# One transformer block on one core: a hand-written instruction order laid out anew

## The chip, the core and the metric

The kernel runs on one core of one Trainium2 chip. Five engines of the core appear below: PE (matrix products; its weight loads are shown as a row of their own, PEld), DVE (vector work), ACT (activation functions), POOL (here only constants) and SP (which issues every DMA). The metric is device time in microseconds. The kernel before was run three times: 169.81, 170.02 and 170.82 us, median 170.02.

## What is computed

A block of two sublayers over x of 2048 rows and 512 columns, in bfloat16. The first sublayer normalises x, forms q, k, v, and does linear attention with 32 heads of 16 columns. The second normalises the result and applies a two-layer network with a ReLU.

```python
phi = lambda t: jnp.where(t > 0, t + 1, jnp.exp(t)) + 1e-6
pq, pk = phi(q), phi(k)
kv  = einsum("bhsd,bhse->bhde", pk, v)
z   = einsum("bhsd->bhd", pk)
o   = einsum("bhqd,bhde->bhqe", pq, kv) / (einsum("bhqd,bhd->bhq", pq, z) + 1e-6)
h   = x + o @ wo                       # q, k, v = layernorm(x) @ wqkv
out = h + relu(layernorm(h) @ w1) @ w2 # w1: 512 x 1792, w2: 1792 x 512
```

## The kernel before

Rows are cut into 16 tiles of 128 rows (t = 0 to 15) and 4 chunks of four tiles (c = 0 to 3). PSUM has 8 banks, and every matrix product names the bank it goes to. Nothing plans the work: a string, ORDER, lists 547 words, and the program emits one small function for each word in the order of the string. A word is a name and its numbers; for products the bank is among them. Each engine runs its own words in the order in which they stand; words of different engines meet only through semaphores, where one reads what another wrote or overwrites what another reads. So an order is a queue for each engine, and a word that must wait holds everything behind it on its engine. SP's queue is one of them: loads, transposing DMAs and stores stand in one line.

```python
for word in ORDER.split():
    name, *idx = word.split(".")
    ops[name](*map(int, idx))
```

The stages and the names that are used below (lines of the profile in brackets):

- **Start.** `lx.t.n` loads n tiles of x, `lk`, `lq`, `lv`, `lo`, `l1`, `l2` load parts of the weights (first number: where the part begins, second: how many slices; all on SP, L201 and L204). `warm` and `warmf` are filler products on zeros (L215, L221). `const` and `masks` fill constants, `table` loads ACT's function table.
- **First normalisation.** `S.t` statistics (DVE, L237), `A.t` aggregates them (DVE, L238), `R.t.n` computes 1/sqrt on ACT (two activations, L243 and L244), `N.t` normalises the tile (DVE, L262). The tile is then transposed, for tiles 0 to 3 by PE (`T.t`, L281) and an ACT copy out of PSUM (`E.t`, L291), for the others by a DMA from SP (`X.t`, L302).
- **Keys.** `K.t` is four products of 512 columns (L310; a word with two more numbers is a half of it). phi is made from them by `F` (exp, ACT), `U` (relu, ACT), `M` (minimum, DVE, L335) and `D` (sum, DVE, L338); for the last pair of tiles `W` takes U's and D's place. `G.t` (PE, L362) accumulates normalised-x-transposed times pk in banks 4 to 7 over all tiles, four products a tile, one a bank. The key sum z is accumulated by DVE in `za`, finished by `zf` (L373 to L375), and brought into columns by small products `z.j` (L381), copied by `zc`, spread by `zh`. The G sums are copied by `gA`, and `kv`, `kx`, `m`, `mA` form one 512 x 512 matrix out of wv, kv and wo.
- **Queries.** `Q.c.j` (L318), with `qF`, `qU`, `qM`, `qD`, `qW` as for keys.
- **Division.** `dn.c` (PE, L459) forms the denominators of a chunk, `dnl` and `dnx` (ACT, L465 and L472) their reciprocals, spread over columns. These are transposed by DMA (`dt.t`, L491, SP), one tile of the first two chunks by PE (`rt`, with `rv` or `re`). `dm` (DVE, L495) multiplies them into the queries, `h.t` (PE, L505) applies the matrix, `hD.t` (DVE, L511) adds x.
- **Second normalisation.** `s`, `a`, `r`, `n` (L239, L240, L243, L269) and the transposes `x.t` (SP, L303), one by PE (`t`, `e`). The division by the deviation is put off to the end.
- **Feed-forward.** `p.c.f` (PE, L521) makes one of 14 slices of the hidden layer for a chunk, four products; `pA` (ACT, L527) or `pD` (DVE, L532) applies the ReLU to a pair of banks. `f.t` (PE, L541) is 14 products of a tile with w2, mostly emitted as two words of seven. `fo.t` (DVE, L549) scales and adds h, `fd.t` (SP, L556) stores. Tile 15 is cut into three pieces by columns.

Of the kernel before, what the change touches and what calls it, by code (L numbers as in the profile page):

```python
# [38 lines left out]
p.0.10.3 hD.8 dt.15 s.8 a.6 pD.0.6.2 a.4 pA.0.10.2 n.6 f.1.1.0.7 hD.9 n.7 f.1.1.7.7 s.9 dm.3.0.2 dm.3.2.2 h.11.7  # L39
a.5 n.5 h.12.2 h.15.6 h.14.4 fo.1 h.10.5 hD.11 f.0.7.0.7 hD.12 x.6 a.8 h.13.1 a.9 f.3.3.0.7 f.3.3.7.7 x.7 hD.15  # L40
n.4 hD.14 f.0.7.7.7 x.4 f.2.0.0.7 hD.13 fo.3 x.5 p.1.0.6 s.12 s.11 n.8 hD.10 fo.0 p.1.1.7 a.11 fd.0 p.1.5.3 s.10
pD.1.0.2 f.2.0.7.7 a.12 n.12 n.9 s.14 p.1.4.2 n.11 p.1.8.4 fo.2 p.1.3.1 r.4.4 a.10 a.14 p.1.13.7 p.1.2.0
pD.1.4.2 n.10 x.10 x.11 s.13 p.1.7.2 p.1.9.5 p.1.12.6 a.13 pD.1.2.2 s.15 a.15 pD.1.8.2 n.14 pD.1.12.2 p.1.6.1
n.15 x.9 x.8 pA.1.6.2 f.7.0.0.7 p.1.10.4 fd.1 p.1.11.5 pD.1.10.2 fd.3 f.5.2.0.7 p.2.9.7 p.2.11.5 f.7.0.7.7
f.5.2.7.7 fo.7 p.2.8.6 p.2.10.4 p.2.5.1 pD.2.10.2 p.2.4.0 r.8.4 pA.2.8.2 f.4.4.0.7 fo.5 p.2.2.5 fd.2 pA.2.4.2
p.2.3.6 n.13 f.4.4.7.7 p.2.1.3 x.12 p.2.0.2 f.6.0.0.7 x.14 pA.2.2.2 fo.4 x.13 x.15 p.3.3.7 p.3.7.5 p.3.2.6
r.12.4 p.3.9.4 f.6.0.7.7 pA.2.0.2 p.3.11.1 p.3.8.3 p.3.4.2 fd.4 fd.5 fo.6 pA.3.8.2 pD.3.2.2 p.3.10.0 p.3.5.3
p.3.6.4 pA.3.10.2 fd.7 pA.3.6.2 p.2.6.6 pD.3.4.2 p.2.7.7 pD.2.6.2 p.3.13.5 p.3.1.1 fd.6 p.2.12.6 p.3.0.0
# [543 lines left out]
```

## Time and profile before

| what | us |
|---|---|
| three runs, median | 170.02 |
| the profiled execution, span from first to last instruction | 168.8 |
| PE busy, weight loads busy | 163.1, 78.0 |
| DVE busy, ACT busy, POOL busy | 104.4, 65.1, 4.8 |
| all products L521 (first layer), mean of one | 50.0, 0.379 |
| all products L541 (second layer) | 50.1 |

The profiled execution's own time is not listed apart from its span; the runs' median stands 1.2 us above the span. The granted PE clock is 1.000 over the whole span. In the profile a product's record is longer than the time for which it holds PE, since products are pipelined: a run of twelve shows 2.75 us. A row of the timeline begins with start and length in us from the start of the span; neighbouring instructions of one kind are merged, with their count behind an x. What stands in brackets at a row's end is idle time of the engine before it, and what ended it. The chain that ended last is followed back from the last instruction. In the views of one line, the row of DMA landings counts from the start of SP's issue.

### The profile page before, as it was taken

How to read it: one execution, taken by the hardware profiler on the slowest of the kernel's cores; microseconds unless marked ns; L12 is line 12 of the kernel's file. 1: busy time of each engine (PE TensorE's matmuls, PEld its weight loads, DVE VectorE, ACT ScalarE, POOL GpSimd, SP SyncE). 2: the span in 40 equal slices, each digit the busy share in tenths (PEclk: the TensorE clock that was granted, in tenths of full speed). 3: DMA queues.
4: the chain of work that ended last, by engine and by line, in shares of the span. 5: the costliest groups of instructions: out<-in, count | busy, mean ns of one | idle time of the engine just before them, and what ended most of it. 6: DMA issues, size and time to landing. Idle time of an engine off the chain costs nothing.

```text
span 168.8 us, 2286 instructions
## 1 busy us (share of the span) xinstructions
PE 163.1 (97%) x855; PEld 78.0 (46%) x871; DVE 104.4 (62%) x205; ACT 65.1 (39%) x97; POOL 4.8 (3%) x21
## 2 busy tenths in 40 slices
...
GB/s 112 352 245 97 97 66 124 176 270 378 174 64 65 77 138 87 134 62 95 37 62 0 31 31 122 126 4 0 62 93 0 31 0 4 0 0 93 0 65 94
DMA packets 30491, 15.49 MB, mean 92 GB/s; under 512 B 23184, under 2 KB 29328, under 8 KB 30480
## 3 DMA queue, kind: packets, MB, share of 16 engines
...
q8 instruction: 7, 0.11, 0.3%
...
HBM read 7.86 MB, written 2.10 MB: 59 GB/s over the span
## 4 chain that ended last, share of the span: by engine, by line
PE 85%; DVE 7%; DMA 4%; issue 1%; SPq 0%
PE bk L541 29%; PE bk L521 28%; PE bk L505 8%; PE bk L318 8%; PE bk L362 6%; PE bk L310 4%; DVE st L237 3%; DMA x_nat<-in_A_x_dram 2%; DMA lnT<-h_nat 2%; DVE h_nat L262 2%; PE bk L459 1%; DVE eb L335 1%; PE bk L403 1%; PE bk L415 1%; SPq L201 0%
## 5 line engine op out<-in xcount | busy, mean ns | idle before, releaser
L541 PE MATMUL bk<-w_sb,at 128*128 128x512 bf16 (+2 forms) x247 | 50.1, 355 | 0.3
L521 PE MATMUL bk<-lnT,w_sb 128*128 128x512 bf16 x219 | 50.0, 379 | 0.3
L527 ACT ACTIVATE at<-bk 128x1024 bf16<-128x1024 f32 x14 | 14.2, 1023 | 57.4 <-PE bk L521 57.4
L541 PEld LDWEIGHTS <-at 128*128 128x128 bf16 x252 | 23.6, 98 | 25.4 <-ACT at L527 0.3
L549 DVE SCALAR_TENSOR_TENSOR gT<-bk,rstd,h_nat 128x512 bf16<-128x512 f32 (+2 forms) x18 | 12.2, 689 | 35.7 <-PE bk L541 35.6
L521 PEld LDWEIGHTS <-w_sb 128*128 128x128 bf16 x224 | 21.8, 98 | 25.8
L532 DVE TENSOR_SCALAR at<-bk 128x1024 bf16<-128x1024 f32 x14 | 17.1, 1218 | 12.8 <-PE bk L521 12.6
L328 ACT ACTIVATE eb<-bk 128x1024 bf16<-128x1024 f32 (+1 forms) x18 | 16.6, 928 | 6.6 <-PE bk L310 4.8
L310 PE MATMUL bk<-wk_sb,lnT 128*128 128x512 bf16 x63 | 15.3, 380 | 0.4 <-ACT lnT L291 0.3
L505 PE MATMUL bk<-m_sb,pqs 128*128 128x512 bf16 x63 | 15.4, 380 | 0.1
L318 PE MATMUL bk<-lnT,wq_sb 128*128 128x512 bf16 x61 | 15.1, 379 | 0.1
L362 PE MATMUL bk<-at,h_nat 128*128 128x512 bf16 x55 | 13.5, 379 | 0.1
L331 ACT ACTIVATE rb<-bk 128x1024 bf16<-128x1024 f32 (+1 forms) x14 | 12.5, 904 | 0.3 <-PE bk L310 0.3
L511 DVE TENSOR_TENSOR h_nat<-bk,x_nat 128x512 bf16<-128x512 f32 x16 | 10.5, 680 | 2.9 <-PE bk L505 2.9
L237 DVE BATCH_NORM_STATS2 st<-x_nat 128x6 f32<-128x512 bf16 x16 | 10.8, 680 | 2.4 <-DMA x_nat<-in_A_x_dram 2.4
L239 DVE BATCH_NORM_STATS2 st<-h_nat 128x6 f32<-128x512 bf16 x16 | 10.7, 683 | 0.1
L310 PEld LDWEIGHTS <-lnT 128*128 128x128 bf16 x64 | 6.0, 98 | 8.4 <-ACT lnT L291 1.0
L362 PEld LDWEIGHTS <-h_nat 128*128 128x128 bf16 x64 | 6.2, 98 | 7.4 <-issue 0.2
L505 PEld LDWEIGHTS <-pqs 128*128 128x128 bf16 x64 | 5.9, 98 | 7.9 <-DVE pqs L495 1.8
L318 PEld LDWEIGHTS <-wq_sb 128*128 128x128 bf16 x64 | 5.9, 98 | 6.4
L472 ACT ACTIVATE wk_sb<-ld 128x1024 bf16<-128x1024 f32 x8 | 8.1, 1050 | 0.1
L335 DVE TENSOR_SCALAR eb<-eb 128x1024 bf16<-128x1024 bf16 (+1 forms) x18 | 6.8, 383 | 0.9 <-ACT eb L328 0.9
...
## 6 DMA issues: line engine op xcount, KB each, us to landing
out_dram<-gT SPq DMA_DIRECT2D x15, 128.0 KB, 1.9
...
```

The source lines that it names most:

```text
L237: op_S = lambda t: nc.vector.bn_stats(out=st[:, t, :], in_=x_nat[:, t, :])
L310: nc.tensor.matmul(bk[:, b, :], lhsT=lnT[c][:, kd, j * P : (j + 1) * P], rhs=wk_sb[:, kd, :], start=(kd == 0), stop=(kd == KD - 1),)
L318: nc.tensor.matmul(bk[:, b, :], lhsT=wq_sb[:, kd, j * P : (j + 1) * P], rhs=lnT[c][:, kd, :], start=(kd == 0), stop=(kd == KD - 1),)
L328: nc.scalar.activation(out=buf(eb, kind, i, n), in_=bank(at_bank[kind, i], n), func=ACT.Exp)
L331: nc.scalar.activation(out=buf(rb, kind, i, n), in_=bank(at_bank[kind, i], n), func=ACT.Relu)
L362: nc.tensor.matmul(bk[:, KD + kd, :], lhsT=ln_nat[:, t, kd * P : (kd + 1) * P], rhs=pk(t)[:, 0, :], start=(t == 0), stop=(t == NT - 1),)
L505: nc.tensor.matmul(bk[:, b, :], lhsT=pqs[:, (c * KD + jb) % NQ, j * P : (j + 1) * P], rhs=m_sb[:, jb, :], start=(jb == 0), stop=(jb == KD ...
L521: nc.tensor.matmul(bk[:, b, cols], lhsT=w1_sb[:, kd, f * P : (f + 1) * P], rhs=lnT[c][:, kd, cols], start=(kd == 0), stop=(kd == KD - 1),)
L527: nc.scalar.activation(out=acts[c % 2][:, f : f + n, :], in_=bank(at_bank["p", c, f], n), func=ACT.Relu)
L532: nc.vector.tensor_scalar(out=acts[c % 2][:, f : f + n, :], in0=bank(at_bank["p", c, f], n), scalar1=0.0, scalar2=None, op0=ALU.max,)
L541: nc.tensor.matmul(bk[:, b, 0 : w * P], lhsT=acts[c % 2][:, f, j * P : (j + 1) * P], rhs=w2_sb[:, f, k * P : (k + w) * P], start=(f == 0), ...
L549: nc.vector.scalar_tensor_tensor(out=o_t[:, t % NO, cols], in0=bk[:, at_bank["f", t, k], 0 : w * P], scalar=rstd2[:, t : t + 1], in1=h_nat ...
```

## The change

Only the string ORDER changes. No function, no size and no operand of an operation is touched; each operation occurs as often as before and in the same pieces. What differs is the place of each word, so the queue of each engine, the banks of most products, and the places of the loads in SP's queue. The diff replaces the whole string; these are the parts that the prediction speaks of, first the start and the X transposes:

```diff
-const lx.0.1 lx.1.1 warmf.4.3 warm.1.3 S.0 table A.0 R.0.1 S.1 lx.2.2 lk.0.2 warm.1.3 N.0 A.1 S.2 R.1.1 lk.2.2
-lx.4.2 A.2 T.0.7 E.0 warm.1.3 S.3 R.2.1 K.0.1.0.2 lx.6.2 A.3 R.3.1 K.0.1.2.2 N.1 T.1.5 F.0.1 E.1 N.2 N.3 T.3.2
-lx.8.4 E.3 S.4 S.5 A.4 T.2.5 lx.12.4 lq.0.2 A.5 K.1.0.0.2 R.4.2 S.6 M.0.1 N.5 S.7 N.4 X.5 E.2 U.0.1 D.0.1 K.3.7
-K.1.0.2.2 F.3.1 M.3.1 X.4 K.2.3.0.2 U.3.1 A.7 A.6 K.2.3.2.2 U.1.1 R.6.2 F.2.1 F.1.1 G.0 D.3.1 G.3 S.9 U.2.1 N.7
-N.6 S.8 K.5.1 K.4.0 M.2.1 A.8 A.9 R.8.2 U.4.2 M.1.1 X.7 D.2.1 F.4.2 D.1.1 N.9 S.12 X.6 N.8 X.9 G.2 K.7.3 S.13
-A.12 A.13 G.1 R.12.2 K.6.2 K.9.1 M.4.2 S.10 F.6.2 N.12 D.4.2 S.11 A.10 U.6.2 X.8 M.6.2 N.13 G.4 X.12 K.8.0 A.11
-R.10.2 S.14 D.6.2 G.5 G.6 X.13 N.10 N.11 S.15 F.8.2 M.8.2 X.11 A.15 U.8.2 A.14 D.8.2 R.14.2 G.7 za.2 za.4 K.12.0
-G.9 K.13.1 N.15 N.14 X.10 lq.2.2 K.11.3 F.12.2 K.10.2 M.12.2 U.12.2 F.10.2 masks X.15 X.14 lv.0.2 lv.2.2 l1.0.2
...
+lx.0.1 table const lx.1.1 lx.2.2 lk.0.2 lx.4.2 lk.2.2 warmf.4.2 S.0 A.0 S.1 A.1 lx.6.2 lx.8.4 lv.2.2 lx.12.4 R.0.1 N.0
+R.1.1 N.1 warm.1.2 T.0.1 warm.1.7 T.1.7 E.0 K.0.4.0.2 E.1 K.1.1.0.2 K.0.4.2.2 masks S.2 S.3 A.3 A.2 S.5 R.3.1 R.2.1
+N.3 S.4 N.2 A.5 A.4 T.3.7 K.1.1.2.2 T.2.2 F.0.1 M.0.1 S.6 E.3 R.4.2 N.5 X.5 E.2 U.0.1 warm.1.3 K.3.3 K.2.0.0.2
+K.2.0.2.2 F.3.1 S.7 D.0.1 N.4 U.3.1 M.3.1 A.7 D.3.1 A.6 X.4 F.2.1 R.6.2 U.1.1 F.1.1 U.2.1 S.8 M.2.1 A.8 N.7 S.9 N.6
+D.2.1 A.9 M.1.1 R.8.2 G.0 G.3 K.5.2 K.4.1 F.4.2 U.4.2 D.1.1 N.8 S.12 M.4.2 S.13 D.4.2 N.9 A.13 A.12 lq.2.2 X.7 X.6
+R.12.2 G.2 G.1 K.7.3 K.6.2 F.6.2 U.6.2 X.8 lq.0.2 X.9 S.11 N.12 X.12 S.10 N.13 A.11 A.10 M.6.2 X.13 D.6.2 R.10.2 S.14
+A.14 N.10 S.15 N.11 A.15 G.4 G.5 K.8.0 K.9.1 G.7 K.12.2 K.13.3 F.8.2 U.8.2 R.14.2 F.12.2 U.12.2 G.6 Q.0.1.1 Q.0.0.0
...
```

Then the key sums and the first division:

```diff
-U.10.2 za.6 D.12.2 M.10.2 G.8 za.8 D.10.2 Q.0.1.1 Q.0.0.0 qF.0.0.2 qU.0.0.2 za.10 G.12 K.14.2 K.15.3 Q.0.2.0
-za.12 Q.0.3.1 G.13 F.14.2 G.11 qF.0.2.2 l2.10.4 qM.0.0.2 M.14.2 W.14.2 zf.12 G.10 qD.0.0.2 qM.0.2.2 G.14
-qU.0.2.2 lo.0.2 z.3.1.14 z.2.1.14 G.15 z.1.1.14 z.0.1.14 qD.0.2.2 zc gA.0.2 gA.2.2 Q.1.0.2 zh dn.0.1 Q.1.1.3
...
-Q.1.3.1 qF.1.2.2 m.0.4 m.1.5 rv.2 Q.3.1.7 qW.1.0.2 m.3.6 Q.2.3.2 dt.3 qM.1.2.2 mA.0.2 qW.1.2.2 dt.0 dt.1 m.2.5
...
+M.8.2 D.8.2 za.2 M.12.2 za.4 N.15 N.14 za.6 qF.0.0.2 qU.0.0.2 za.8 lo.2.2 X.10 X.11 K.11.3 K.10.2 F.10.2 U.10.2 D.12.2
+M.10.2 D.10.2 za.10 qM.0.0.2 za.12 l2.3.4 lv.0.2 X.14 X.15 lo.0.2 l2.0.3 l2.7.3 l1.0.2 G.8 Q.0.3.1 G.9 K.14.2 K.15.3
+F.14.2 M.14.2 W.14.2 Q.0.2.0 G.11 G.12 G.10 G.13 G.14 qF.0.2.2 qU.0.2.2 zf.12 qM.0.2.2 qD.0.0.2 qD.0.2.2 z.2.0.14
+z.0.0.14 z.1.0.14 G.15 z.3.0.14 gA.0.2 zc zh Q.1.0.3 gA.2.2 dn.0.5 dnl.0 dnx.0.2.2 Q.1.1.4 kv.1.7 kv.2.7 kv.0.7 kv.3.7
+Q.1.3.1 Q.1.2.0 qF.1.0.2 dnx.0.0.2 kx qM.1.0.2 qW.1.0.2 dt.3 l2.10.4 dt.0 dt.1 qF.1.2.2 Q.2.3.2 m.0.6 m.1.7 rt.2.3
...
+dt.5 dt.4 dt.7 l1.2.2 Q.2.0.6 Q.3.2.0 h.2.2 Q.3.3.1 re.6 qF.3.0.2 qU.3.0.2 qU.2.0.2 qF.2.0.2 qF.3.2.2 dm.1.0.2
...
```

Then the second division, the places in the feed-forward part, and the end:

```diff
-p.0.13.7 p.0.1.6 p.0.8.2 p.0.9.3 dnx.2.0.2 qD.3.0.2 s.4 l2.7.3 p.0.11.4 pA.0.0.2 dt.11 l2.0.3 dt.9 dt.10 r.0.4
-qM.3.2.2 qW.3.2.2 s.6 dt.8 p.0.12.6 s.7 pD.0.12.2 p.0.3.1 p.0.2.0 pA.0.8.2 dn.3.2 p.0.5.7 dnl.3 p.0.4.6 a.7
-dm.2.0.2 pA.0.2.2 dnx.3.0.2 dnx.3.2.2 dm.2.2.2 pD.0.4.2 h.9.0 h.8.5 p.0.6.6 p.0.7.7 dt.13 dt.12 s.5 dt.14
...
-fo.15.3.1 fo.8 f.12.1.7.7 fd.9 f.13.4.7.7 fd.8 f.15.0.0.14.0.2 fo.14 fo.12 fd.12 fo.13 fd.15.3.1 fo.15.0.2
-f.15.5.0.14.2.1 fd.13 fd.14 fd.15.0.2 fo.15.2.1 fd.15.2.1
...
+qM.3.2.2 qW.3.2.2 qD.3.0.2 x.3 x.1 x.0 e.2 dnl.2 dnx.2.2.2 p.0.8.2 p.0.3.4 p.0.2.3 p.0.7.5 p.0.1.7 dn.3.1 dnx.2.0.2
+pA.0.2.2 r.0.4 dnl.3 dt.10 dt.9 dt.8 dt.11 p.0.9.3 p.0.6.4 s.4 s.6 a.6 hD.7 a.4 n.4 s.7 pD.0.6.2 dm.2.0.2 dm.2.2.2
+dnx.3.0.2 dnx.3.2.2 p.0.0.6 pA.0.0.2 pA.0.8.2 p.0.5.1 p.0.4.0 h.9.5 p.0.13.4 h.8.6 h.10.2 p.0.12.3 a.7 s.5 pD.0.4.2
...
+a.8 hD.11 n.7 s.9 dm.3.0.2 dm.3.2.2 f.2.3.7.7 h.12.5 h.15.1 x.6 x.7 x.5 x.4 s.10 s.11 a.10 n.10 hD.12 a.11 fo.2 a.9
+h.13.0 h.14.2 p.1.5.6 hD.15 s.15 a.15 n.8 hD.13 hD.14 n.11 s.13 s.14 p.1.2.1 p.1.4.5 pD.1.4.2 f.1.3.0.7 p.1.11.7
...
+p.1.7.5 f.0.6.0.7 p.1.1.1 pA.1.6.2 p.1.0.0 pD.1.0.2 f.0.6.7.7 p.1.12.1 fo.0 x.10 x.9 fd.2 x.13 x.8 x.15 p.1.9.4
...
+p.3.13.1 p.3.12.0 pA.3.12.2 f.15.5.0.14.0.2 p.2.11.3 p.2.10.2 fo.15.0.2 fo.6 pD.2.10.2 fd.5 fd.6 p.2.9.5 p.2.13.1
...
+fo.12 fd.11 fd.12 fd.10 fo.9 fd.9 f.15.4.0.14.2.1 fo.15.2.1 fd.15.2.1 f.15.2.0.14.3.1 fo.15.3.1 fd.15.3.1
```

More of the change, by code (lines that the diff above doesn't have):

```diff
@@ L34 @@
-Q.3.3.1 x.3 dm.1.2.2 qF.3.0.2 hD.2 n.1 s.2 Q.3.2.0 qU.2.0.2 qF.2.0.2 h.5.2 h.6.3 a.2 qU.3.0.2 qM.2.0.2 h.4.7 n.2
-qF.3.2.2 x.0 qD.2.0.2 t.2.5 qD.2.2.2 hD.4 x.1 hD.6 h.7.4 dn.2.6 hD.5 hD.7 e.2 dnl.2 qM.3.0.2 p.0.0.5 dnx.2.2.2
-p.0.13.7 p.0.1.6 p.0.8.2 p.0.9.3 dnx.2.0.2 qD.3.0.2 s.4 l2.7.3 p.0.11.4 pA.0.0.2 dt.11 l2.0.3 dt.9 dt.10 r.0.4
-qM.3.2.2 qW.3.2.2 s.6 dt.8 p.0.12.6 s.7 pD.0.12.2 p.0.3.1 p.0.2.0 pA.0.8.2 dn.3.2 p.0.5.7 dnl.3 p.0.4.6 a.7
-dm.2.0.2 pA.0.2.2 dnx.3.0.2 dnx.3.2.2 dm.2.2.2 pD.0.4.2 h.9.0 h.8.5 p.0.6.6 p.0.7.7 dt.13 dt.12 s.5 dt.14
@@ L39 @@
[L39 to L48, printed above, removed]
```

16 lines of the change are left out of this document (11 added, 5 removed).

## The prediction

> **What bounds the kernel now.** I read the page first, then a table of stretches, then the chain that ended last, then the timeline of the first 13 us engine by engine.
>
> ```profile
> span 168.8 us, 2286 instructions
> PE 163.1 (97%) x855; PEld 78.0 (46%) x871; DVE 104.4 (62%) x205; ACT 65.1 (39%) x97; POOL 4.8 (3%) x21
> ```
> ```profile
> 5.60:12.10 6.50, 5.68 (x34) 2.77 (x33) 6.43 (x18) 5.45 (x15) 0.57 (x2) 1.00 0.82 308
> 12.10:21.10 9.00, 8.81 (x41) 3.74 (x40) 9.00 (x30) 7.24 (x15) 0.00 (x0) 1.00 0.53 103
> 21.10:39.20 18.10, 18.00 (x82) 8.24 (x85) 17.21 (x29) 11.71 (x16) 0.00 (x0) 1.00 0.73 174
> ```
> ```profile
> 17.65 3.40 DMA lnT<-h_nat
> ...
> 21.10 1.04 PE bk L310 x4
> ...
> 166.18 0.35 DVE gT L549
> ```
>
> The page says PE. The stretches (length, then busy us of PE, weight loads, DVE, ACT, POOL) say more: DVE is busy 6.43 of 6.50, 9.00 of 9.00 and 17.21 of 18.10 us, so up to 39.2 us PE and DVE are both full. The chain agrees: DVE in front, one DMA transpose (X.8) at 17.65, then PE from 21.10 to 166.2. Both orders hold 547 words with the same counts of every operation and piece, so PE's own sum is unchanged. The time can move only by PE's waits, and before 39.2 us not by more than DVE moves.
>
> **Part 1, tile 1 ahead of the statistics of tiles 2 and 3.**
>
> ```profile
> 3.94 0.66 DVE L237 BATCH_NORM_STATS2 st<-x_nat 128x6 f32<-128x512 bf16 x1
> 4.63 0.41 DVE L262 TENSOR_SCALAR h_nat<-x_nat,mv,rstd 128x512 bf16<-128x512 bf16 x1
> 4.96 0.18 DVE L238 BATCH_NORM_AGGREGATE mv<-st 128x2 f32<-128x6 f32 x1
> 5.60 0.70 DVE L237 BATCH_NORM_STATS2 st<-x_nat 128x6 f32<-128x512 bf16 x1 [0.47 <-DMA x_nat<-in_A_x_dram]
> ...
> 7.23 1.09 DVE L262 TENSOR_SCALAR h_nat<-x_nat,mv,rstd 128x512 bf16<-128x512 bf16 x3
> 8.24 1.28 DVE L237 BATCH_NORM_STATS2 st<-x_nat 128x6 f32<-128x512 bf16 x2
> ```
> ```profile
> 5.17 0.29 ACT L243 ACTIVATE rstd<-mv,eps 128x1 f32<-128x1 f32 x1 [0.57 <-DVE mv L238]
> 5.49 0.20 ACT L244 ACTIVATE rstd<-rstd 128x1 f32<-128x1 f32 x1
> 6.34 0.60 ACT L291 ACTIVATE lnT<-bk 128x512 bf16<-128x512 bf16 x1 [0.64 <-PE bk L281]
> ```
>
> A.1 now runs right behind S.1, at 4.63 in place of 4.96; N.0 follows 0.10 later than before, 4.73 to 5.14. R.1 moves up by 0.33, to 4.84, and ends at 5.36 (0.52 for its two activations), so N.1 runs from 5.40 (7.23 before) to 5.81. It lies in the 0.47 us in which DVE waited for tiles 2 and 3. N.1 holds its queue for about 0.33 (1.09 for three, 0.41 for one), so S.2 starts at 5.72, 0.12 late, but with 0.33 of work done: **DVE is 0.2 us ahead**. Should tiles 2 and 3 land later (they are issued third, as before), N.1 is covered all the more.
>
> ```profile
> 5.67 0.63 PE L281 MATMUL bk<-ident,h_nat 128*128 128x128 bf16 x4
> ...
> 6.99 1.05 PE L310 MATMUL bk<-wk_sb,lnT 128*128 128x512 bf16 x4 [0.26 <-ACT lnT L291]
> ...
> 9.43 2.75 PE L310 MATMUL bk<-wk_sb,lnT 128*128 128x512 bf16 x12
> 12.13 1.02 PE L362 MATMUL bk<-pk_lo,h_nat 128*128 128x512 bf16 x4
> ```
>
> A full matmul holds PE for 0.216 (2.75 us for 12, of which the last shows 0.38), a group of four 0.863. One filler, not two, now stands ahead of T.0, so T.0 starts about 5.30 (5.67), E.0 ends about 6.57, and K.0's first half starts 6.62 (6.99). T.1 starts 6.16, E.1 ends 7.43; K.1's first half runs from 7.48 and K.0's second half to 8.34. On DVE, with 0.6 a statistic (1.28 for two), S.5 starts 7.2, N.3 7.88 (its R.3 stands behind E.1), N.2 8.80. T.3 is at 8.4, K.1 ends 9.05, T.2 is at 9.25. Then E.3 (ends 9.62) and E.2 (10.5, behind R.4) release K.3 at 9.7 and K.2 at 10.56 to 11.42, where the old order ended its 12 matmuls at 12.02. D.0 comes behind S.7 at 11.04 and ends 11.46, so G.0 starts at 11.5 (12.13): 0.6 ahead.
>
> That shrinks at once. G.3 needs D.3, which ends 12.43, and K.4 needs X.4's DMA transpose.
>
> ```profile
> 10.42 0.41 DVE L262 TENSOR_SCALAR h_nat<-x_nat,mv,rstd 128x512 bf16<-128x512 bf16 x1
> ```
> ```profile
> L302 SPq DMA_TRANSPOSE lnT<-h_nat x12: 1188/1208/1282, 10.9 to 28.9; - x12
> ...
> DMA to landing us min/median/max: 2.4/2.5/4.1
> ```
>
> SP issues one transpose in 1.2 to 1.3 us, and it lands 2.5 after the start of its issue. N.5 ends 10.50 (10.83); X.5 and X.4 are issued 10.53 and 11.92; X.4 lands 14.4 and K.4 starts 14.42. Before it was 14.72 (12.13 and three groups): **0.3 ahead**.
>
> **Part 2, DVE up to the key sums.**
>
> ```profile
> 28.41 0.43 DVE L335 TENSOR_SCALAR eb<-eb 128x1024 bf16<-128x1024 bf16 x1 [0.53 <-ACT eb L328]
> ...
> 37.09 0.68 DVE L373 TENSOR_TENSOR at<-at 128x512 f32<-128x512 f32 x1
> ...
> 38.27 0.69 DVE L375 TENSOR_TENSOR at<-at 128x512 bf16<-128x512 f32 x1
> ```
> ```profile
> 39.24 0.34 PE L381 MATMUL bk<-ones,at 128*128 128x1 bf16 x8
> ```
>
> The work ahead of zf is the same list in both orders and DVE stays full, so zf ends 0.25 earlier, 38.7 (38.96), and at most 0.5 earlier still if the wait of 0.53 goes too. PE reaches z.2 at 38.6 (28 groups after K.4) and waits for zf to 38.8. Three z's stand ahead of G.15 now, two before: the same matmuls. Q.1.0 would start at 40.05; before, 39.24 and the z's and G.15 put it at 40.5. **0.45 ahead**, and never more than the 0.2 + 0.53 that DVE can give.
>
> **Part 3, loads that SP now carries between.** lq.2 stands ahead of X.7 and lq.0 ahead of X.9; both were elsewhere. A load's bytes stand ahead of the transpose. The nearest row is in the second division, where a 384 KB load was issued just ahead of three transposes; first the load, then they:
>
> ```profile
> DMA to landing us min/median/max: 3.7/3.7/3.7
> ```
> ```profile
> L491 SPq DMA_TRANSPOSE rd<-wk_sb x3: 1188/1264/1270, 65.7 to 68.3; - x3
> ...
> DMA to landing us min/median/max: 2.5/2.7/3.5
> ```
>
> The first took 1.0 longer than 2.5, the second 0.2, the last nothing; the first came half a us behind the load (65.0 + 3.7 against 65.7 + 3.5). For 256 KB I take two thirds or less, 0.1 to 0.7. By SP's queue X.7 lands 16.6 for K.7 at 17.0 (three groups after K.4), X.9 21.0 for K.9 at 21.3 (eight), and X.13, issued about 21.0, 23.5 for K.13 at 23.9 (eleven). All fit by 0.3 to 0.4. But of the old twelve one took 3.4 and one 4.1; at X.9 or X.13 this is 0.5 to 1.2 us of PE. I take 0.1, nearest to the median, and keep 0 and 1.2. Left: Q.1.0 at 40.15, **0.35 ahead**. The masks move ahead in the program, on POOL, which waits for nothing either way: 0.
>
> **Part 4, l2.10.4 between dt.3 and dt.0.**
>
> ```profile
> 42.35 1.06 ACT L472 ACTIVATE wk_sb<-ld 128x1024 bf16<-128x1024 f32 x1
> 44.21 1.05 ACT L472 ACTIVATE wk_sb<-ld 128x1024 bf16<-128x1024 f32 x1
> 49.50 1.29 DVE L495 TENSOR_TENSOR pqs<-pqT,rd 128x1024 bf16<-128x1024 bf16 x2 [1.02 <-DMA rd<-wk_sb]
> 50.25 2.07 PE L505 MATMUL bk<-m_sb,pqs 128*128 128x512 bf16 x8
> 71.62 2.07 PE L505 MATMUL bk<-m_sb,pqs 128*128 128x512 bf16 x8
> ```
> ```profile
> x_nat<-in_A_x_dram SPq DMA_DIRECT2D x2, 128.0 KB, 2.3
> ```
>
> DVE's multiply dm.0 waits for transposes of the reciprocals, and h.3 waits for dm.0: eight matmuls should show 1.89 and show 2.07, so 0.18 is lost, here and once more at 71.62. The two reciprocals now end 0.35 earlier, 43.05 and 44.9. dt.3 is issued 43.1, l2.10.4 44.3, dt.0 44.9, dt.1 46.15. From 128 KB in 2.3 and 384 KB in 3.7, I estimate 4.4 for its 512 KB: landing 48.7. dt.0 and dt.1 follow half a us apart, 49.2 and 49.6; dm.0 starts 49.65 (49.50), and h.3 loses what it was ahead. Bounds: 0.35 ahead stays if the load costs nothing (dt.1 at 48.6); 0.75 behind if dt.1 takes 4.1. I take **0**: the start's gain ends here.
>
> The Trainium skill, page "DMA: Bandwidth & Descriptors", section on the anatomy of one DMA (measured on the gpsimd path), fits a DMA as 2.0 us plus its bytes over 436 KB per us. By that, an estimate of 3.2 us for this load, the sum would keep the 0.35; but it makes 2.9 of the 384 KB whose row shows 3.7, so the row decides.
>
> **Part 5, the second division and the rest.** Before, a load stood among dt.11, 9, 10 and 8; now dt.10, 9, 8, 11 follow each other from about 63.3 (dnx.2 is where it was), the last lands about 69.6 (68.3 + 2.5 = 70.8 before), dm.2 is done 70.9. h.9 stands one group earlier in PE's queue, 70.6, and has its first operand by 70.3: **-0.18**, bounds -0.18 and +0.3 (a relu evacuation stands just ahead of dm.2 on DVE).
>
> ```profile
> 61.64 7.93 PE L521 MATMUL bk<-lnT,w_sb 128*128 128x512 bf16 x35
> ```
> ```profile
> L532 DVE TENSOR_SCALAR at<-bk 128x1024 bf16<-128x1024 f32 x14 | 17.1, 1218 | 12.8 <-PE bk L521 12.6 <-remote 0.2
> L527 ACT ACTIVATE at<-bk 128x1024 bf16<-128x1024 f32 x14 | 14.2, 1023 | 57.4 <-PE bk L521 57.4
> ```
>
> l1.2.2 now comes behind dt.7, at 54.5, ahead of x.3, x.1 and x.0. Its 896 KB by the same slope take 4.9 to 6.6 us; x.0, issued 58.5, lands 61.0 undelayed, and the first p at 61.64 needs it: 0, bounds 0 and 0.5. The feed-forward part is ordered anew, but nearly every bank is emptied (1.22 by DVE, 1.02 by ACT) under two groups or more. Two places are bare: p.1.12 needs bank 1 from pD.1.0, 1.22 and some 0.25 around it under the 1.51 of f.0.6.7.7; the first piece of f.15 needs pA.3.12, 1.02 under 1.3. Together 0.05, bounds 0 and 0.4. p.1 starts 7.5 us earlier in PE's queue and needs x.4, which I place at 82.9 against 84.0: 0, bounds 0 and 0.5. The tail ends as before in a short piece, one 0.35 us multiply-add and a store.
>
> Sum: 0 (start, spent at h.3) - 0.18 + 0.05 = -0.13, span 168.7. The median of the runs is 170.02, 1.2 above the profiled span; with that kept, **169.9 us**.
>
> **Rivals.** *Slower: PE waits for a late transpose.* Place: X.13 for K.13, which PE now reaches 2.4 us sooner while SP issues X.13 no sooner. It decides from a landing of 2.9 us on. At the row's 4.1 it costs 1.2, X.9's at 3.4 costs 0.5, and zf and h.3 come as much later, less the 0.3 of part 1: 171.4; with x.4's 0.5, 171.9. For: room of 0.3 to 0.4, and two such landings in twelve. Against: the median of 2.5. *Faster: all 1.83 us by which N.1 moves reaches the end*, 168.2. For: the chain runs through the start. Against: DVE can give 0.2 + 0.53 and the two divisions 0.18 each, so 168.9 is the floor. *The clock.* T.0's four matmuls took 0.63, 0.107 apart, K.0's 0.216 for four times the columns: PE doubled its speed between the two. The new K.0 and K.1 start earlier; if the change came behind them, eight matmuls at 0.43 cost 1.7, half of it under the waits for E.1 and N.3: 170.8. The Trainium skill ("TensorE: Matmul & The Clock Gate", Part 1) has the gate judge by a free-running window of 3.4 us and calls the number of slow matmuls variable from run to run; the trace has one sample.
>
> **How the numbers follow.** The forecast 0.76, within 1%, which is about what a measurement of this kernel can tell from no change; late transposes 0.15, of which 0.10 beyond 1%; N.1's whole gain 0.04; the clock 0.05, of which 0.02 beyond. So faster 0.04, same 0.84, slower 0.12. Low end: the floor, 168.9. High end: 171.3, nearly the rival's 171.4.
>
> **What would show it.** N.1 near 5.4, G.0 near 11.5, zf's end near 38.7, DVE waiting for rd to about 49.6, no loss at h.9. I am wrong if PE waits over 0.5 us on lnT at K.9, K.13 or p.1, if p's wait for banks, or if h.3 keeps its lead.

## The result, and the profile after

Four executions of the changed kernel took 172.28 to 173.40 us, median 173.0; the kernel before took 170.38 (median of four). The ratio is 1.0158, with a 95% interval of 1.0118 to 1.0197: slower by more than 1%, and outside the range forecast. The profiled execution after took 172.28 with a span of 170.6. It is the fastest of its four, so the two traces, 168.84 and 170.57, show 1.73 us of the 2.6 between the medians. Ratios, here and below, leave out an execution over 1.5% above the fastest of its kernel, which concerns one of e10 and two of e11.

The page, the table by stages, the chain of waits and the list of waits, after (the stages and their columns are those of the prediction):

```profile
span 170.6 us, 2314 instructions
PE 163.7 (96%) x871; PEld 77.2 (45%) x871; DVE 104.8 (61%) x205; ACT 65.1 (38%) x97; POOL 4.9 (3%) x21
```
```profile
5.60:12.10 6.50, 5.78 (x33) 2.28 (x33) 6.44 (x19) 5.45 (x15) 0.61 (x2) 1.00 0.85 300
12.10:21.10 9.00, 8.97 (x42) 3.78 (x41) 8.93 (x29) 6.89 (x15) 0.00 (x0) 1.00 0.64 143
21.10:39.20 18.10, 17.38 (x82) 7.64 (x81) 16.88 (x28) 11.49 (x16) 0.00 (x0) 1.00 0.81 208
```
```profile
18.79 3.51 DMA lnT<-h_nat
22.35 1.04 PE bk L308 x4
...
41.05 0.89 PE bk L316 x4
...
47.30 3.44 DMA rd<-wk_sb
51.69 2.93 PE bk L503 x12
...
63.22 4.33 PE bk L519 x20
...
165.08 2.24 DMA out_dram<-gT
```
```profile
DVE pqs L493 <- DMA rd<-wk_sb: 1.9, 1, 1.9
PE bk L503 <- DVE pqs L493: 0.9, 1, 0.9
PE bk L308 <- DMA lnT<-h_nat: 0.7, 1, 0.7
```

In the chain of before one DMA stood between DVE's start and PE's end. Now three do, and at each PE or the tail waits: the transpose X.9 (lnT) ahead of K.9, the transpose dt.1 (rd) ahead of DVE's dm.0 and PE's h.3, and the store of tile 11 in the tail. The third stage shows PE 17.38 busy of 18.10, where before it was 18.00. Line numbers are 2 less than before.

The balance along PE, each place against the trace of before: K.4 0.17 us ahead (14.55 against 14.72); K.9 starts at 22.35 and has lost 0.88, of which before lost 0.30 at K.8; Q.1.0 0.54 behind (41.05 against 40.51); h.3 1.44 behind (51.69 against 50.25); the last matmul 1.19 behind (167.34 against 166.14), since h.9 and what follows it lose less than before; the end of the span 1.73 behind, since from PE's last matmul to the end are 3.24 us in place of 2.70.

### The profile page after: what moved, and what is told of

The parts are those of the page before. It is cut to its first block, busy times and chain, and to the rows that moved or that the text cites. A ratio compares the mean times of both kernels' runs of the same rounds, so it can differ in the third digit from the quotient of the medians.

```text
span 170.6 us, 2314 instructions
## 1 busy us (share of the span) xinstructions
PE 163.7 (96%) x871; PEld 77.2 (45%) x871; DVE 104.8 (61%) x205; ACT 65.1 (38%) x97; POOL 4.9 (3%) x21
## 4 chain that ended last, share of the span: by engine, by line
PE 80%; DVE 9%; DMA 7%; issue 1%; ACT 1%; DVEq 0%; SPq 0%
PE bk L519 28%; PE bk L539 27%; PE bk L503 8%; PE bk L316 6%; PE bk L360 5%; DVE st L235 4%; PE bk L308 4%; DMA lnT<-h_nat 2%; DMA rd<-wk_sb 2%; DMA out_dram<-gT 1%; DMA x_nat<-in_A_x_dram 1%; DVE h_nat L260 1%; DVE at L336 1%; PE bk L457 1%; DVE gT L547 1%
## 5 line engine op out<-in xcount | busy, mean ns | idle before, releaser
L519 PE MATMUL bk<-lnT,w_sb 128*128 128x512 bf16 x224 | 50.6, 379 | 0.0
L308 PE MATMUL bk<-wk_sb,lnT 128*128 128x512 bf16 x64 | 16.0, 380 | 1.3 <-DMA lnT<-h_nat 0.7
L316 PE MATMUL bk<-lnT,wq_sb 128*128 128x512 bf16 x64 | 15.6, 379 | 0.0
L241 ACT ACTIVATE rstd<-mv,eps 128x2 f32<-128x2 f32 (+2 forms) x14 | 4.1, 294 | 15.5 <-DVE mv L238 10.9
```

The costliest lines, as they stand in the source:

```text
L308: nc.tensor.matmul(bk[:, b, :], lhsT=lnT[c][:, kd, j * P : (j + 1) * P], rhs=wk_sb[:, kd, :], start=(kd == 0), stop=(kd == KD - 1),)
L316: nc.tensor.matmul(bk[:, b, :], lhsT=wq_sb[:, kd, j * P : (j + 1) * P], rhs=lnT[c][:, kd, :], start=(kd == 0), stop=(kd == KD - 1),)
L519: nc.tensor.matmul(bk[:, b, cols], lhsT=w1_sb[:, kd, f * P : (f + 1) * P], rhs=lnT[c][:, kd, cols], start=(kd == 0), stop=(kd == KD - 1),)
```

## The experiments

Theory at first: loads set ahead of transposes in SP's queue (lq.0 ahead of X.9, l2.10.4 ahead of dt.0 and dt.1) and the store of tile 11 hold the whole loss. Rival: the order itself needs its transposes sooner than they come, and the loads are innocent. Kernels named e1 to e17 differ from the changed kernel or the one before in the words shown. Ratios are to the kernel before, with 95% intervals.

**e1: lq.0 away from X.9.** (In the changed kernel X.9 took 3.51 us, and K.9 lost 0.88.)

```diff
-lx.8.4 lv.2.2 lx.12.4
+lx.8.4 lq.0.2 lx.12.4
...
-X.8 lq.0.2 X.9
+X.8 X.9
...
-lv.0.2 X.14
+lv.0.2 lv.2.2 X.14
```

> The changed kernel with lq.0 moved from ahead of X.9 to the early place of lv.2, and lv.2 set beside lv.0. Theory (a load just ahead of a transpose in SP's queue makes the transpose land late): X.9 lands 2.5 to 2.8 us after its issue, near 21.4 in place of 22.30, K.9 waits 0.1 us or less in place of 0.7, zf ends near 39.0 (39.66), h.3 starts near 51.0 (51.69); the time is 0.7 us below the changed kernel's, 1.011 to 1.012 of the kernel before (1.0158). Rival (the new order brings K.9 forward to where any transpose of its length comes late, and X.9's 3.5 us is an instruction fetch among its packets): X.9 still takes 3.3 us or more, K.9 still waits 0.5 us, the ratio stays 1.016.

Ratio 1.017 [1.0149, 1.0191], as after. The view of X.9 alone, e1:

```profile
L300 SPq DMA_TRANSPOSE lnT<-h_nat x1: 1189/1189/1189, 18.6 to 18.6; - x1
...
DMA to landing us min/median/max: 3.4/3.4/3.4
```

With no load near it X.9 still takes 3.4 us, K.9 still loses 0.74 of the 0.88, and now X.13 (4.07) makes K.13 lose 0.76 as well. For K.9 the theory falls; the rival's "an instruction fetch among its packets" remains.

**e2: l2.10.4 behind dt.1. e3: tiles 10 and 11 exchanged in the tail. e4: these two and e1.**

```diff
-dt.3 l2.10.4 dt.0 dt.1
+dt.3 dt.0 dt.1 l2.10.4
...
-f.10.0.0.7 f.14.2.7.7 f.11.1.0.7 f.10.0.7.7 f.9.5.0.7 f.11.1.7.7
+f.11.0.0.7 f.14.2.7.7 f.10.1.0.7 f.11.0.7.7 f.9.5.0.7 f.10.1.7.7
...
-fo.10 fo.11 fo.12 fd.11 fd.12 fd.10
+fo.11 fd.11 fo.10 fo.12 fd.12 fd.10
```

> The changed kernel with l2.10.4 moved from between dt.3 and dt.0 to behind dt.1. Theory (the 512 KB ahead of dt.0 and dt.1 hold up their bytes): dt.1 lands near 49.5 in place of 50.75, dm.0 starts near 49.8 in place of 50.94, h.3 loses 0.3 us or less in place of 1.25, and the time is 0.9 to 1.0 us below the changed kernel's, about 1.010 of the kernel before. Rival (the reciprocals and dt.3 come late because PE and ACT are half a us behind, the load is innocent): dt.1 lands after 50.4, h.3 stays within 0.3 of 51.69, the ratio stays 1.015 to 1.016.

> The changed kernel with tiles 10 and 11 exchanged in the tail, so that tile 11's store, whose buffer the pieces of tile 15 use again, is issued some 3 us sooner. Theory (tile 15's piece waited for that store): the store of 11 lands before 164.8, the multiply-add of piece 15.2 starts within 0.2 us of its matmuls' end or of the one before it on DVE, near 166.9 in place of 167.44; from PE's last matmul to the end of the span 2.8 to 2.9 us in place of 3.24; the time 0.35 us below, 1.0137 of the kernel before. Rival (the tail is set by the last store's own issue and landing): 3.1 to 3.3 us from PE's end to the end, no difference in time.

> The changed kernel with the three edits together: lq.0 early, l2.10.4 behind dt.1, tiles 10 and 11 exchanged in the tail. Theory (these three places hold the whole loss): the gains add up, 0.7 + 1.0 + 0.35 = about 2 us below the changed kernel, a span near 168.6, 1.000 to 1.005 of the kernel before. Rival (the new order is slower in itself, so that what one edit gives back another wait takes): less than half of it, 1.010 or more of the kernel before, with PE waiting for lnT or rd at some other word.

e2: 1.0111 [1.0088, 1.0133]. dm.0 and h.3 in the timeline of e2, and the three transposes dt.3, dt.0 and dt.1 there; then the same two views of after:

```profile
49.87 1.30 DVE L493 TENSOR_TENSOR pqs<-pqT,rd 128x1024 bf16<-128x1024 bf16 x2 [0.70 <-DMA rd<-wk_sb]
50.77 2.57 PE L503 MATMUL bk<-m_sb,pqs 128*128 128x512 bf16 x11
```
```profile
DMA to landing us min/median/max: 2.4/2.5/3.0
```
```profile
50.94 1.29 DVE L493 TENSOR_TENSOR pqs<-pqT,rd 128x1024 bf16<-128x1024 bf16 x2 [1.94 <-DMA rd<-wk_sb]
51.69 0.60 PE L503 MATMUL bk<-m_sb,pqs 128*128 128x512 bf16 x2 [0.93 <-DVE pqs L493]
```
```profile
DMA to landing us min/median/max: 2.6/3.4/4.1
```

Though K.9 lost more in e2 (1.07), h.3 loses nothing and starts 0.92 us sooner: the load's cost is shown. Of that 0.45 is lost again at p.0, where x.3, issued behind l1.2.2, takes 4.8 us.

e3: 1.013 [1.011, 1.0149]. The tail of DVE, e3:

```profile
165.03 2.64 DVE L547 SCALAR_TENSOR_TENSOR gT<-bk,rstd,h_nat 128x512 bf16<-128x512 f32 x4 [2.22 <-PE bk L539]
168.10 0.35 DVE L547 SCALAR_TENSOR_TENSOR gT<-bk,rstd,h_nat 128x128 bf16<-128x128 f32 x1 [0.43 <-PE bk L539]
```

The first of the two pieces of tile 15 is now the fourth of an unbroken row of DVE (after, DVE stood 0.88 us ahead of it). From PE's end to the end are 2.99 us, in e4 2.72.

e4: 1.0095 [1.0074, 1.0116], 1.1 us below the changed kernel, where 2 were expected. h.3 and the tail are clean, but K.9 loses 0.77 and K.13 0.84: the rest of the loss lies at X.9 and X.13.

**The instruction packets.** The DMA view lists packets of a kind of its own. The page of after; the stretches of 0.1 us from 20.5 and from 23.6, after; the stretch from 22.8 in before, and the view of X.13 there:

```profile
q8 instruction: 7, 0.11, 0.3%
q14 instruction: 4, 0.03, 0.1%
```
```profile
q14 instruction: 1, 0.01, 29.8%
...
q8 instruction: 1, 0.02, 108.2%
```
```profile
q8 instruction: 1, 0.02, 54.8%
```
```profile
DMA to landing us min/median/max: 4.1/4.1/4.1
```

Those of q8 are single packets of 16 KB, those of q14 of 8 KB. By the records of the packets they took 0.3 to 1.9 us each, where a transpose's own pieces of 256 bytes take 0.02. In after the q8 packets fall where 94, 223, 351, 469, 600, 713 and 841 matmuls have started, about 128 apart: this reads as PE's program, fetched while it runs. The Trainium skill ("Trainium Architecture — The Big Picture", section on the software stack) has instructions of 64 bytes; by estimate 16 KB are then 256, which agrees with 128 matmuls and their weight loads. That section has the streams brought in when the program is loaded; the trace shows packets of them during the run. New theory: X.9 met the one of 20.5 us (X.8, in before, one at 19.5), and X.13, in e1, the one of 23.25.

**e5 to e8: moving the packets, and the start alone.** On top of e4, e5 sets 8 memsets of 128x1 on DVE behind const; e6 makes the 8 float32 warm-ups of 256 columns 4 of 512; e7 has both, and l1.2.2 behind l1.0.2. e8 is the kernel before with the change's words up to K.2.0.2.2.

```diff
-const lx.1.1
+const pad.8 lx.1.1
...
-warmf.4.2
+warmg.2.2
...
-dt.7 l1.2.2
+dt.7
...
-l1.0.2 G.8
+l1.0.2 l1.2.2 G.8
```

> The kernel with the three edits, and 8 memsets of one element per partition on DVE at its start, where it waits for the first tile of x. They do nothing but move the point at which DVE's 8 KB instruction fetch (20.48 us there) is issued some eight DVE instructions earlier. New theory (X.9 lands late because that fetch lies among its packets, whatever load stands ahead of it): the fetch comes near 17.2 us, X.9 takes 2.5 to 2.8 us and lands near 21.3, K.9 waits 0.1 us or less in place of 0.77. K.13 then still waits, since PE's own 16 KB fetch follows PE and still lies among the packets of X.13 or X.12. Time: the gain of K.9 is mostly spent at K.13, 0 to 0.7 us below the run with three edits (1.0095): 1.005 to 1.0095. Rival (X.9 is late by its place, issued 18.6 us and behind X.8): the fetch moves or not, X.9 still takes 3.3 us or more and K.9 still waits 0.7.

> The kernel with the three edits, and the 8 float32 warm-up matmuls of 256 columns at PE's start made 4 of 512 columns: the same work in 4 matmuls and 4 weight loads fewer, so that PE's first 16 KB instruction fetch (23.29 us there) comes 4 matmuls, 0.8 to 0.9 us, later. New theory: the fetch comes near 24.1, behind the packets of X.13; X.13 takes 2.5 to 2.8 us in place of 4.24 and lands near 23.8, K.13 waits 0.1 us or less in place of 0.84; K.9 still waits 0.7. Time 0.7 to 0.8 us below the run with three edits: about 1.005 of the kernel before. Rival (X.13 is late by its place in SP's queue): X.13 still takes about 4.2 us and K.13 still waits 0.8, ratio 1.0095.

> Both shifts of the fetches on top of the three edits, and l1.2.2 moved from ahead of x.3, x.1 and x.0 to behind l1.0.2, where SP and the DMA engines are free. New theory: K.9 and K.13 both wait 0.1 us or less (1.6 us together before), p.0 doesn't wait for x.3; PE's first 16 KB fetch now lies some 0.5 us earlier than with the PE shift alone (K.9 isn't held), so X.13 is free of it only narrowly. Span 168.0 to 168.3 in place of 169.6, ratio 0.998 to 1.002: level with the kernel before or a little below it. Rival (the new order needs these transposes sooner than SP can give them, fetch or none): PE waits at K.9 and K.13 for 0.7 us or more in sum, ratio 1.005 or more.

> The kernel before with the changed kernel's start alone (loads, tiles 0 to 7's statistics, normalisations, transposes on PE and the first four key products, in the order of the change; lq.0 in the place of lv.2), then the rest of the order of before. Theory of the prediction: PE and DVE are 0.2 to 0.3 us ahead at K.4, and that is spent or kept at the first wait for a DMA transpose; 0 to 0.3 us below the kernel before, ratio 0.998 to 1.000. New theory adds: the fetches follow the engines, so X.8's (3.4 us of before) or X.13's (4.1) lateness moves with them and the 0.5 us lost there in all can become 0.2 to 1.2: ratio 0.997 to 1.004. Rival (tile 1 ahead in itself costs what the changed kernel lost): 1.006 or more.

e5: 1.0081 [1.0065, 1.0096]. The 8 KB packet moved from 20.48 to 18.58. X.9 alone, then X.12 and X.13, e5:

```profile
L300 SPq DMA_TRANSPOSE lnT<-h_nat x1: 1192/1192/1192, 18.8 to 18.8; - x1
...
DMA to landing us min/median/max: 2.3/2.3/2.3
...
L300 SPq DMA_TRANSPOSE lnT<-h_nat x2: 1217/1217/1217, 20.1 to 21.4; - x2
...
DMA to landing us min/median/max: 2.4/3.2/4.1
```

X.9, issued at 18.82 in place of 18.64 and with nothing but the memsets changed, falls from 3.4 to 2.3 us and K.9 no longer waits: its wait was the packet. The packet now meets X.8 (3.3), which has room. K.13 takes the gain back, 1.73, as expected.

e6: 1.0153 [1.0132, 1.0173], expected 1.005: a miss. The 16 KB packet moved by 0.4 us only, to 23.69, X.13 took 4.48, and K.13 lost 1.08. e7: 1.0126 [1.0104, 1.0149], a miss again: no loss at K.9 or p.0, but X.13 took 4.13 and K.13 lost 1.37; and PE's last packet, at 165.57, fell among the last stores, with 3.99 us from PE's end to the end. e8: 0.9998 [0.9984, 1.0011]: the new start by itself is worth nothing that can be measured, and costs nothing.

**e9 to e11: 26 matmuls more, ahead of all work.** Warm-ups of 128 columns in bfloat16, 34 in place of 8 in float32 (4 in e7), fill the same time at PE's start, and the 8 memsets of e5 stand on DVE; this on the run of e7 (e9), on the changed kernel (e10) and on the kernel before (e11). The edit is that of e10.

```diff
-warmf.4.2
+warmq.34.2
```

> The kernel with the three edits, the 8 idle memsets on DVE, l1.2.2 behind l1.0.2, and PE's 8 warm-up matmuls of 256 float32 columns made 34 of 128 bf16 columns (about 3.6 us of warm-up in place of 3.4): 26 more matmuls ahead of the real ones, so every 16 KB fetch of PE (one per 128 matmuls) comes 26 matmuls, about 5.6 us, earlier in the work. Theory of the fetches: the first falls near 17, behind X.6 and X.8, which have room; X.9 and X.13 take 2.3 to 2.8 us, K.9 and K.13 wait 0.1 us or less (0.77 and 0.84 in the run with three edits, 1.37 at K.13 in the last one); the last falls near 159, 7 us ahead of the last matmul, and from PE's end to the end are 2.6 to 2.8 us. Span 167.7 to 168.1, ratio 0.993 to 0.998: below the kernel before. Rival (X.13 stands too late in SP's queue, the fetch only coincides): X.13 takes 4 us again, K.13 waits 0.8 or more, ratio 1.003 or more.

> The changed kernel, its order untouched, with the 8 memsets and the 34 short warm-ups alone. Theory of the fetches: of the changed kernel's loss K.9's 0.88 goes and K.13 doesn't take its place (0.1 or less), the store of tile 11 lands in 1.8 us in place of 2.24 and the tail gives back 0.3 of 0.54; l2.10.4 still holds up dt.0 and dt.1, so h.3 still loses 0.9 to 1.2 us. In sum 1.0 to 1.3 us below the changed kernel: ratio 1.008 to 1.010 in place of 1.0158. Rival (the order itself is what costs): 1.014 or more.

> The kernel before, its order untouched, with the same 8 memsets and 34 short warm-ups. Theory of the fetches: X.8 (3.4 us) and X.13 (4.1) take 2.3 to 2.8, PE's 0.3 and 0.2 us at K.8 and behind it go; but PE's third fetch moves from 63.6 to near 58, among x.3, x.1 and x.0, where before it stood behind them, and can cost up to 1 us at the first p. Ratio 0.997 to 1.004. So a change of nothing but warm-up instructions can move the kernel before either way by as much as many an edit. Rival (the fetches cost the kernel before nothing): 0.999 to 1.001 with all of its waits in place.

All three ratios missed, upward: 1.0149 [1.0128, 1.017], 1.0287 [1.0241, 1.0333] and 1.0221 [1.017, 1.0272]. The first packet did come some 6 us sooner, but it wasn't harmless. X.4, X.7, X.6 and X.8 of e9, issued 11.9 to 16.4, with the stretch from 16.2:

```profile
L300 SPq DMA_TRANSPOSE lnT<-h_nat x4: 1189/1211/2567, 11.9 to 16.4; - x4
...
DMA to landing us min/median/max: 2.4/4.7/5.2
```
```profile
q8 instruction: 1, 0.02, 104.6%
```

Three transposes behind one another took 5.2, 5.0 and 4.4 us, and K.7 lost 2.14 (e10 2.24; e11 2.01, at K.6). The new warm-up also left PE slow for longer (T.1's four products start 0.107 us apart in e9, 0.06 in after), but that isn't K.7's loss: X.7 was issued at 13.82, in e7 at 13.86. I had expected the packet near 17 us, behind X.6 and X.8 and where they have room. X.9 and X.13, which the packet had left, took 2.3 and 2.4 us without a wait in e9: that part held. In e10 PE's granted clock fell as well, right behind K.7's wait; its page:

```profile
PEclk9999789999999999999999999999999999999999
```

The clock was 0.50 from 19.9 to 23.3 us there. The three executions of e10 with a mean clock of 1.000 took 173.97 to 174.88 us, the three with 0.981 to 0.988 took 176.00 to 178.25: part of its 1.0287 is this.

And the kernel before, its order untouched, became some 2% slower (172.06 to 175.05 us, five of six above 174.4) by 26 matmuls and 8 memsets that do nothing: about as much as the whole change cost. Its trace shows three places: K.6 loses 2.01, p.0 1.09 and h.12 1.52, each behind a transpose (X.6 took 5.1 us, x.1 3.8, dt.15 4.3) with a PE packet in its time (17.2, 60.2 and 80.8 us).

**e12 to e17: the new order clear of packets.** All start from e4 with l1.2.2 early, and all set one of tile 15's two last pieces ahead of the second half of tile 9. e12 to e14 keep the 8 memsets. e12 has the PE packet later (7 matmuls fewer); e13 sets N.9 behind N.8, and N.12 and N.13 ahead of S.11, so that X.13 is issued 0.6 us sooner, with 4 matmuls fewer; e14 the same with the usual warm-up. In these three the matmuls of that piece overwrite tile 13's bank before DVE has read it, so tile 13 comes out wrong and DVE stalls in the tail; only what lies ahead of it is read.

```diff
-N.8 S.12 M.4.2 S.13 D.4.2 N.9 A.13 A.12
+N.8 N.9 S.12 S.13 A.13 A.12 R.12.2 M.4.2 D.4.2 N.12 N.13
```

> The kernel with the three edits, the 8 memsets on DVE and l1.2.2 early, now with PE's fetches later: 4 warm-up matmuls of 512 float32 columns and without the three single fillers between the first transposes (7 matmuls fewer in all), and in the tail one of tile 15's two last pieces set ahead of the second half of tile 9, so that PE's last fetch falls some 4 us ahead of the last matmul. Theory of the fetches: the first falls near 23.8, behind the last packet of X.13 (23.4); X.13 takes 2.3 to 2.6 us, K.9 and K.13 wait 0.1 us or less, the tail is 2.7 us: span 167.9 to 168.4, time 0.996 to 1.000 of the kernel before. Rival (the new order is short of time at X.13 by itself): X.13 takes 4 us again, K.13 waits 0.8 or more, 1.003 or more.

> As the last one, but with the three fillers back (4 matmuls fewer than the changed kernel), and on DVE N.9 behind N.8, N.12 and N.13 ahead of S.11, so that X.9, X.12 and X.13 are issued some 1.0, 0.7 and 0.7 us sooner. Theory of the fetches: X.13's last packets are through by 22.7 and PE's first fetch falls near 23.1: X.9, X.12, X.13 take 2.3 to 2.8 us, no wait at K.9, K.12, K.13; span 167.7 to 168.2, 0.995 to 0.999 of the kernel before. Rival (DVE's order matters, not the fetch: what N.13 gains, M.4, D.4 and the stages behind lose): zf ends later than 39.3 and Q.1.0 waits, 1.000 or more.

> As the last one, with the changed kernel's own warm-up: nothing differs but PE's matmul count before its first fetch. Theory of the fetches: it falls near 22.3, in the last packets of X.13 (issued near 20.7); X.13 takes 3.3 us or more and lands near 24.2 to 24.8, K.13, wanted at 23.9, waits 0.3 to 0.9; 0.3 to 0.9 us above the last kernel. Rival: no difference from the last kernel beyond 0.2 us, and X.13 takes 2.5 us.

Their whole times, 1.028 to 1.039, say nothing. e12: the packet at 23.48 again met X.13 (3.89), K.13 lost 1.37. e13, X.8, X.9, X.12 and X.13:

```profile
L300 SPq DMA_TRANSPOSE lnT<-h_nat x4: 1190/1217/1217, 16.5 to 20.8; - x4
...
DMA to landing us min/median/max: 2.3/2.3/2.4
```

No wait from K.9 to K.13. But the 8 KB packet now fell at 15.73, X.7 took 3.7 (4.0 in e14) and K.7 lost 0.69 (0.95). In e14 PE's packet fell at 20.88, not near 22.3, on X.12 (3.9), which had room; X.13 took 3.1. So e14 doesn't tell what it was made for.

e15 is that order with tile 13 read in time, without memsets; e16 the same with 12 of them; e17 is e16 with lq.2 moved from ahead of X.7 to behind X.8.

> The order of the last kernel (three edits, l1.2.2 early, N.9, N.12 and N.13 sooner on DVE), with tile 13's multiply-add put back ahead of the matmuls that use its bank again, and without the 8 memsets, so that DVE's 8 KB fetch, which in the last two fell at 15.7 us on X.7 (3.7 to 4.0 us, K.7 waited 0.7 to 0.95), comes 8 instructions, some 2 to 3 us, later, between X.8 and X.9, which have room. Theory of the fetches: no wait over 0.2 us at K.7, K.9, K.12 or K.13, none at h.3, p.0 or in the tail; PE's last matmul ends at 164.8 to 165.4 (166.1 in the profile of before) and the span is 167.4 to 168.1: 0.993 to 0.998 of the kernel before. Rival (one of the transposes is late in any case, whatever the fetch): a wait of 0.7 us or more stays among K.7 to K.13, 0.999 or more.

> As the last one, with 12 memsets on DVE, 4 more than in the kernels whose fetch fell on X.7: its 8 KB fetch comes 1 to 2 us sooner, near 14, on lq.2 or X.4's last packets. Theory of the fetches: X.7 takes 2.5 to 3.2 us, K.7 waits 0.3 us or less, and the span lies within 0.4 us of the last kernel's. Rival (memsets on DVE at the start cost or gain by themselves, or X.7 is late because lq.2 stands ahead of it): K.7 waits 0.7 us or more again, 0.5 to 0.9 us above the last kernel.

> As the last kernel (fetch near 15.8 us, X.7 3.9 us, K.7 waiting 0.61), with lq.2 moved from ahead of X.7 to between X.8 and X.9. Theory: X.7 is issued near 13.2 and lands near 15.7, before DVE's fetch; the fetch then falls on X.6 or X.8, which have room; X.9 lands near 21.0 for K.9 at 21.3 or a little later. No wait over 0.2 us from K.7 to K.13; the span falls by 0.4 to 0.6 us to 168.0 to 168.2, and the time to 0.997 to 1.000 of the kernel before: level with it or just below. Rival (what K.7 gives back is taken by X.9 behind the load, or by DVE, which is full up to zf): no gain, 1.001 to 1.003.

e15: 1.0023 [1.0006, 1.0039]; e16: 1.0016 [1.0005, 1.0027]; e17: 1.0033 [1.0018, 1.0048]. X.7 in e15, in e16 and in e17:

```profile
DMA to landing us min/median/max: 3.0/3.0/3.0
```
```profile
DMA to landing us min/median/max: 3.9/3.9/3.9
```
```profile
DMA to landing us min/median/max: 2.9/2.9/2.9
```

With lq.2 ahead and the packet elsewhere (e15, at 20.47) X.7 takes 3.0 and K.7 doesn't wait; with both (e16, packet at 15.80) 3.9, and K.7 loses 0.61; without lq.2 (e17, packet at 14.77) 2.9 and no wait. So K.7's wait needs both. In e17 PE's packet came back to X.13 (3.86, at 22.67) and K.13 lost 0.50. e16 is the nearest that the new order came: 2.4 us below the changed kernel, still 0.3 above the one before. e15 and e17 had been expected at 0.993 to 0.998 and 0.997 to 1.000, and e16's K.7 without a wait: three misses. No run passed the kernel before.

**All transposes together.** The 19 profiles hold 779 transposes. Sorted by whether an instruction packet was moving between 1.0 us after the issue and 0.5 us before the landing, and whether an earlier load or store was still under way 1.05 us after the issue:

| in its time | transposes | median us | of 3.3 us or more |
|---|---|---|---|
| neither | 504 | 2.44 | 0 |
| a load or store ahead | 153 | 2.64 | 21 |
| an instruction packet | 91 | 3.05 | 36 |
| both | 31 | 3.72 | 28 |

No transpose with neither of them took over 3.05 us. (A late transpose has more time in which to meet a packet; with the same 2.3 us from the issue for all of them, one late transpose, X.13 of e6, falls into the first row.) The Trainium skill ("DMA: Bandwidth & Descriptors", section on queues, rings and completion order) has each DMA engine take turns between its queues by whole packets. By that a packet would hold one of the 16 engines, and a transpose with pieces on it would land late; the table and e5 agree. The size doesn't follow: beside one 8 KB packet, recorded as 0.31 to 0.59 us, X.9 (e1, e4, e6) and X.8 (before, e5, e8) came 0.9 to 1.0 us over the median, and X.13 beside one of 16 KB, 0.88 to 1.17 us, came 1.2 to 2.0 over it (before, e1, e4, e6, e8). What holds them beyond the packet's record is not shown.

## Why the prediction was wrong, by its own steps

**Part 1, right.** N.1 ran at 5.37 (5.40 forecast), G.0 started at 11.64 (11.5), K.4 0.17 ahead (0.3). e8 gives the price, in the order of before: none that can be measured. That the start brings nothing to the end was right; its lead was gone at K.9 already, not at h.3. The rival by which all 1.83 us of N.1 reach the end falls with it, and so does that of the clock: T.0's four products took 0.40 us in after (0.63 in before), so PE had its full speed ahead of K.0, not behind K.1.

**Part 2, wrong as a consequence.** "zf ends 0.25 earlier, 38.7": it ended at 39.66. The two waits of DVE ahead of it, 0.24 at M.8 and 0.49 at D.8, are those for the exponential and the relu of K.8 and K.9.

**Part 3, the first failed step: "I take 0.1, nearest to the median, and keep 0 and 1.2".** It cost 0.88 at K.9, inside the bounds and over the 0.5 that the prediction names as a sign of being wrong, and hardly by the load on which the step was argued (0.74 without it, e1). X.9 was issued at 18.79 and would have landed at 21.1 to 21.3 undisturbed, as e5 shows, in time. The trace of before had the answer: I read "of the old twelve one took 3.4 and one 4.1" as scatter with a chance, and didn't ask what lay beside those two. The DMA view shows an instruction packet at each, at 19.5 and 22.85 us.

**Part 4, the second: "I take 0", h.3 at the old time.** The load's landing was right, 4.4 us estimated and 4.29 measured (45.39 to 49.68). By the formula of the Trainium skill ("DMA: Bandwidth & Descriptors", section on the anatomy of one DMA), which it gives for the gpsimd path, it would have been, by estimate, 3.2; the measurement decides, on this queue. dt.0 landed 0.51 and dt.1 1.07 behind the load, nearly the half us apart that was forecast. What failed is the room: the load was to spend the 0.35 by which PE was ahead, but Q.1.0 was 0.54 behind since K.9's loss came first, so that the load was issued at 45.39, not 44.3, and dt.1 at 47.30, not 46.15. dt.1 landed at 50.75, not 49.6, and h.3 fell back by another 0.90; e2 gives 0.92 back. The bounds, from 0.35 ahead to 0.75 behind, leave 1.1 for the load, so its cost was inside them; the choice of 0 needed everything ahead of it to hold.

**Part 5, mostly right.** The later stages gave 0.25 back (1.44 to 1.19 behind), where 0.18 was forecast (the other 0.07 was not traced), and the bare places in the feed-forward part cost nothing. l1.2.2 cost nothing only because h.3 was late: in e2 0.45 shows, the forecast bound.

**The tail, the third: "The tail ends as before".** It had no bound at all, and cost 0.54. I compared the kind of the last piece and not the buffers: o_t has four places, tile 15 uses tile 11's, and the new order stores tile 11 at 165.08, 2.3 us ahead of PE's end, in place of well before. With an instruction packet at 165.05 beside it that store took 2.24 us (1.8 in e10, without one). e3 and e4 give 0.25 and 0.52 back.

**The rival** "PE waits for a late transpose" was the right one, with the wrong first place (X.13; it named X.9 too) and too small a chance. Its 171.4 lacked h.3's further loss and the tail. The median of 173.0 lies 1.7 above the range's high end: 0.5 of it is the mechanism (span 170.57 and the 1.2 of the sum give 171.8), 0.5 the distance from span to time, which was 1.7 in that execution, and 0.7 is that this execution was the fastest of four. Taken together: -0.17 ahead at K.4, 0.7 by Q.1.0, 0.9 to h.3, -0.25 behind it, 0.54 in the tail, 1.73 in all.

**What stays open.** What sets the place of a packet to better than 1 to 3 us: the first of PE came at 22.4, 24.3 and 20.9 us in kernels that differ by 0 to 4 matmuls (e5, e13, e14), so it also hangs on how far the engine's queue runs ahead of its waits. That the 8 KB packet near 20 us is DVE's own program is argued from the memsets that move it (e4 to e5, 20.48 to 18.58; e15 to e16, 20.47 to 15.80), not shown. In e6 PE's packet begins 2.45 us after X.13's issue, when others have landed, and X.13 still takes 4.48. And the last 0.3 us of e16 has K.7's 0.61 in it, which I didn't get rid of without a new wait.
